# An adaptive-layernorm block on one Trainium2 core: matmuls of zeros in the opening, c loaded in rows, and another order of work in chunk 2

## The chip, the core and the metric

The kernel runs on one core of a Trainium2 chip. The core has five engines that run their own instruction streams: TensorE (PE in the profile; its weight loads are PEld), VectorE (DVE), ScalarE (ACT), GpSimd (POOL) and SyncE (SP), which here only issues transfers. TensorE writes its results to PSUM, eight banks from which VectorE and ScalarE read; everything else on the chip lies in SBUF. The engines wait for each other through semaphores, and each works through its own queue in order. The metric is the device time of one execution in microseconds (us).

## What is computed

A block with adaptive layernorm: from a condition row c six modulation rows are made; then a dilated sliding-window attention (32 heads of 18, eight keys two positions apart) and a gated feed-forward without a nonlinearity, each on a modulated layernorm and each added back through a gate row. 2048 rows of 576 values, bf16.

```python
mod = (silu(c) @ w_mod).reshape(1, 6, 1, -1)          # c (1, 576), w_mod (576, 3456)
sa, ca, ga, sb, cb, gb = (mod[:, k] for k in range(6))
h = layernorm(x) * (1 + ca) + sa
x = x + ga * A(h)                                     # A: wqkv (576, 1728), wo (576, 576)
h = layernorm(x) * (1 + cb) + sb
x = x + gb * B(h)

def A(x):                                             # W, dil = 8, 2
    q, k, v = split_heads(x @ wqkv)                   # 32 heads of 18
    idx = arange(S)[:, None] - arange(W) * dil        # masked where idx < 0
    attn = softmax(einsum(q, k[idx]) * 18 ** -0.5)
    return einsum(attn, v[idx]) @ wo

def B(x):                                             # w_gate, w_up (576, 4608), w_down (4608, 576)
    return ((x @ w_gate) * (x @ w_up)) @ w_down
```

## The kernel before

**Tiling.** The rows are cut into eight chunks of 256 (`CH`), each of two halves (`ST` = 2, index `j`) of 128 rows. The 576 columns are five tiles of 128 (`KT`); the fifth overlaps or is padded. The feed-forward works on five groups of row tiles, `GROUPS`: tiles 0 to 1 (chunk 0 alone), then 2 to 5, 6 to 9, 10 to 12, 13 to 15. For each group `gate_up` streams w_gate and w_up in nine blocks of 512 columns, and `down` streams w_down.

**Order.** Everything is under a manual schedule (`tc.manual_schedule`): each engine carries out its instructions in the order in which the Python text issues them. The order of the opening is written out by hand at the end of the main function; from the first `gate_up` on, attention for later chunks is spread as background pieces between the feed-forward's matmuls.

**The opening.** The steps up to the first feed-forward matmul are:

- Loads go out on SyncE in one order: x of chunk 0 by halves (L176), the weights of modulation rows 0 and 1 (`wmA`, through `load_wm` and `load_k`, L167 and L168), three pieces of wqk, x of chunk 1, wv, x of chunk 2, modulation rows 3 and 4 (`wmB`, four loads), wo in four pieces (L816), modulation row 2 (`wmC`, in a tile of the pool `wd`), x again for the residual, the rows 512 to 575 of w_gate and w_up (`wgr`), and five feed-forward blocks (L149). c is loaded on ScalarE's queue straight into columns, one value per partition (L183, L184).
- c is turned to silu(c) by Exp on ScalarE (L750) and three small VectorE operations (L754 to L756), giving `sc`. `ln_parts` makes the layernorm of a chunk in parts: `stat` (L233, L235) on VectorE, `rsq` (L238, L239) on ScalarE, `norm` (L243) on VectorE.
- `transposed` turns normalised rows by ten matmuls with the identity (L270) into PSUM; its result, when called, writes them with scale and shift to `hT` or `h2T`, three of five tiles on one of VectorE and ScalarE, two on the other (L259, L261).
- `mod_columns(wmA, 0)` computes two modulation rows as columns: two blocks of 25 matmuls with one moving column (L283), then VectorE adds into `modc` (L286, L288). `mod_row` computes the gate row `ga` for all partitions by ten matmuls (L295), and ScalarE copies it to `ga_bc` (L297, L298).
- `a_qj(j, g)` makes Q and K of one half of chunk 0, 45 matmuls of 128 columns a half (L338); `a_q(i, g)` makes group g of chunk i in matmuls of 256 columns, 45 in five groups. ScalarE copies both to qT and kT (L341 to L346). `a_v(i, j)` makes the value rows (L364, L366), ScalarE copies them (L368, L369), and GpSimd's queue writes them to DRAM (`vd`, L375), from where `b_ld` loads the shifted windows `vsh` (L383).
- Chunk 0's attention is done on its own path: products q·k on VectorE (`pj`, L778), sums per head on TensorE (`lj`, L786), softmax (`max_j`, `sum_j`), weights shifted to key positions by `to_keys` (L481 to L487, ScalarE copying `keyed`), weighted values on VectorE (`av_mul`, L496, four instructions), and their sums on TensorE (`av_sum(j, hf)`, L507, twenty matmuls a call into three PSUM tiles `po`). After the second call of a half ScalarE copies them to `oT` (L510 to L512).
- `b_wj(j)` multiplies half j by Wo (L521); `x1_half`, its result, forms the new residual x1 on VectorE (L527, L528) with the statistics of the second layernorm, whose rstd is `rsq2` and whose rows are `norm2`. Two calls of `transposed` write `h2T`, and then `gate_up` of group 0 begins (L621).

**PSUM.** In the opening a pool of five banks (`psp0`, tag "bank", function `ps`) serves everything but the `po` tiles, which have a pool of three (`pop`). Before the first feed-forward both pools are closed and one of eight banks is opened over them, so that the first tile of the new pool waits for the work of the old ones.

Of the kernel before, what the change touches and what calls it, by code (L numbers as in the profile page):

```python
# [7 lines left out]
BF = mybir.dt.bfloat16  # L8
F32 = mybir.dt.float32
ALU = mybir.AluOpType  # L10
# [33 lines left out]
def kernel(  # L44
# [49 lines left out]
    def js(j):  # L94
        return slice(j * P, (j + 1) * P)
# [75 lines left out]
    def load_wm(wm, bi, blk):  # L171
        return load_k(lambda p, k: wm[p, k, bi, :], w_mod, blk * D, D)

    x_in[0] = sp.tile([P, ST, D], BF, name="x_t0")
    for j in range(ST):
        nc.sync.dma_start(x_in[0][:, j, :], x_flat[js(j), :])  # L176
    c_bf = sp.tile([P, KT], BF, name="c_bf")
    nc.vector.memset(c_bf[:], 0.0)
    nc.vector.memset(eps[:], EPS)
    nc.vector.memset(addc[:, 0, :], 0.0)  # L180
    nc.vector.memset(addc[:, 1, :], 1.0)
    with nc.allow_non_contiguous_dma(reason="tiny column-layout load of c"):
        nc.scalar.dma_start(c_bf[:, 0:KF], c[0, 0:KF * P].rearrange("(m p) -> p m", p=P))  # L183
        nc.scalar.dma_start(c_bf[0:64, KF:KT], c[0, KF * P:D].rearrange("(m p) -> p m", p=64))  # L184
    nc.scalar.preload_act_table_set("natural_log_exp_and_others")
    wmA = sp.tile([P, KT, 2, D], BF, name="wmA", tag="wm")
    wmC = wdp.tile([P, FB, D], BF, name="wd")
    wmCr = x1p.tile([P, D], BF, name="x1")
# [8 lines left out]
    load_k(lambda p, k: wv[p, k, :], A_wqkv, 2 * D, D)  # L197


    nc.gpsimd.memset(ident[:], 0.0)  # L200
    nc.gpsimd.affine_select(out=ident[:], in_=ident[:], compare_op=ALU.not_equal, fill=1.0, base=0,
                            pattern=[[-1, P]], channel_multiplier=1)
    nc.gpsimd.memset(wqk[64:, KF, :], 0.0)
    for k in range(2):
        nc.gpsimd.memset(kTs[k][64:, KF, :], 0.0)
# [41 lines left out]
    def layernorm(src, tag):  # L247
        xn, stat, rsq, norm = ln_parts(src, tag)
        for j in range(ST):
            stat(j)  # L250

        def norms():
            for j in range(ST):
                norm(j)
        return xn, lambda: rsq(slice(0, ST)), norms

# [6 lines left out]
    def transposed(src, dst, cols, vi):  # L263
        n = P * len(cols)
        pA = ps([P, 3, n], BF, "tr_pA")
        pB = ps([P, 2, n], BF, "tr_pB")
        for m in range(KT):
            d = pA[:, m, :] if m < 3 else pB[:, m - 3, :]
            for c, j in enumerate(cols):
                nc.tensor.transpose(d[:, js(c)], src[:, j, m * P:(m + 1) * P], ident[:])  # L270

        def evict(first_on_dve=True):
            for m in range(KT):
                s = pA[:, m, :] if m < 3 else pB[:, m - 3, :]
                modulate(dst(m), s, m, vi + 1, vi, (m < 3) == first_on_dve)
        return evict

    def mod_columns(wm, pi):
        pm = ps([P, 2, KT], F32, "pm")
        for bi in range(2):  # L280
            for kt in range(KT):
                for m in range(KT):
                    nc.tensor.matmul(pm[:, bi, m:m + 1], lhsT=wm[:, kt, bi, col(m)], rhs=sc[:, kt:kt + 1],  # L283
                                     start=(bi == 0 and kt == 0 and m == 0), stop=(kt == KT - 1), skip_group_check=True)
        c01 = slice(2 * pi, 2 * pi + 2)
        nc.vector.tensor_tensor(modc[:, c01, 0:KF], pm[:, :, 0:KF], addc[:, :, 0:KF], ALU.add)  # L286
        for r in (slice(0, 64), slice(64, P)):
            nc.vector.tensor_tensor(modc[r, c01, KF:KT], pm[64:P, :, KF:KT], addc[64:P, :, KF:KT], ALU.add)  # L288

    def mod_row(wm, dst, sc_bc):  # L290
        pa = ps([P, 512], F32, "pa")
        pb = ps([P, 64], F32, "pb")
        for p_t, c0, c1 in ((pa, 0, 512), (pb, 512, D)):
            for kt in range(KT):
                nc.tensor.matmul(p_t[:], lhsT=sc_bc[:, kt, :], rhs=wm(slice(0, P), kt)[:, c0:c1],  # L295
                                 start=(kt == 0), stop=(kt == KT - 1))
        nc.scalar.copy(dst[:, 0:512], pa[:])  # L297
        nc.scalar.copy(dst[:, 512:D], pb[:])  # L298
# [49 lines left out]
    def a_q(i, g):  # L348
        qk_tiles(i, QGRP[g], slice(0, CH), nc.scalar.copy)
        if g == 2:  # L350
            a_halo(i)
# [394 lines left out]
    x0 = x_in.pop(0)  # L746
    xn0, stat0, rsq0, norm0 = ln_parts(lambda j: x0[:, j, :], "a")
    aa[0] = dict(xn=xn0)
    e_f = sp.tile([P, KT], F32, name="e_f")
    nc.scalar.activation(e_f[:], c_bf[:], ACTF.Exp, scale=-1.0)  # L750
    for j in range(ST):
        stat0(j)
        rsq0(slice(j, j + 1))
    nc.vector.tensor_scalar_add(e_f[:], e_f[:], 1.0)  # L754
    nc.vector.reciprocal(e_f[:], e_f[:])
    nc.vector.tensor_tensor(sc[:], c_bf[:], e_f[:], ALU.mult)  # L756
    for j in range(ST):
        norm0(j)
    a_tiles(0)
    a_halo(0)  # L760
    hT0 = aa[0]["hT"]
    nc.gpsimd.tensor_copy(sc_bc[:], sc[:, :, None].to_broadcast([P, KT, P]))
    ev = [transposed(xn0, lambda m, j=j: hT0[:, m, js(j)], (j,), 0) for j in range(ST)]
    mod_columns(wmA, 0)
    for e in ev:
        e()
    for j, g in ((0, 0), (1, 0), (0, 1), (0, 2), (1, 1), (1, 2)):
        a_qj(j, g, nc.scalar.copy)
    a_ln(1)
# [28 lines left out]
    def sum_j(j):  # L798
        ss = small.tile([P, H], F32, name="ssj")
        nc.vector.tensor_reduce(ss[:], dd0[:, j].rearrange("p w h -> p h w"), axis=AX.X, op=ALU.add)  # L800
        nc.vector.reciprocal(ss[:], ss[:])
        nc.vector.tensor_tensor(attn0[:, :, j], dd0[:, j].rearrange("p (a w) h -> p a w h", a=2),
                                ss[:, None, None, :].to_broadcast([P, 2, 4, H]), ALU.mult)

    def behind(dma, load):
        tc.add_manual_dep(dma.ins, load.ins.name, SYNC, reason="value rows go first")
# [1 line left out]
    load_x(2)  # L808
    wmB = sp.tile([P, KT, 2, D], BF, name="wmB", tag="wm")
    nc.gpsimd.memset(wmB[64:, KF, :, :], 0.0)  # L810
    load_wm(wmB, 0, 3)
    load_wm(wmB, 1, 4)
    for dd4 in range(4):
        nk = (DH - dd4 + 3) // 4
        wsrc = bass.AP(A_wo.tensor, A_wo.offset + dd4 * D, [[DH * D, H], [4 * D, nk], [1, D]])
# [40 lines left out]
    max_j(1)  # L856
    a_q(1, 4)
    mod_columns(wmB, 1)
    aa[2]["norm"]()
    sum_j(1)  # L860
    for j in range(ST):
        a_v(1, j)
    a_t(2, False)
    mod_row(lambda p, k: wmC[p, k, :] if k < KF else wmCr[p, :], ga_bc, sc_bc)
    for j in range(ST):
        to_keys(j)
    av_mul(0, 0)
    av_mul(0, 1)
    a_q(2, 0)
    av_sum(0, 0)  # L870
    av_mul(1, 0)
    a_q(2, 1)
    av_sum(0, 1)
    av_mul(1, 1)
    xn2, stat2, rsq2, norm2 = ln_parts(lambda j: x1[0][j], "b")
    ht, _ = h2_of(0)
    av_sum(1, 0)
    x1_half = b_wj(0)
    x1_half(stat2)
    rsq2(slice(0, 1))  # L880
    a_q(2, 2)
    av_sum(1, 1)
    norm2(0)
    a_q(2, 3)
    x1_half = b_wj(1)
    x1_half(stat2)
    rsq2(slice(1, 2))
    transposed(xn2, lambda m: ht[:, m, js(0)], (0,), 2)()
    norm2(1)
    a_q(2, 4)  # L890
    for j in range(ST):
        a_v(2, j)
    transposed(xn2, lambda m: ht[:, m, js(1)], (1,), 2)()
    behind(b_ld(1, 0), wgu_in[3])
    behind(b_ld(1, 1), wgu_in[4])
    load_res(1)
# [75 lines left out]
```

## Time and profile before

| | us |
|---|---|
| Time, median of 3 runs (lowest, highest) | 569.56 (569.03, 569.99) |
| The profiled execution, its own time | 569.6 |
| Its span, first to last instruction | 567.7 |
| TensorE busy (share of the span) | 547.7 (96%) |
| TensorE weight loads busy | 325.1 (57%) |
| VectorE busy | 327.9 (58%) |
| ScalarE busy | 250.4 (44%) |
| GpSimd busy | 69.5 (12%) |
| First matmul | 6.32 |
| First Q/K matmul of chunk 0 | 11.79 |
| First value matmul of chunk 0 | 19.51 |
| First feed-forward matmul | 57.39 |

All positions are counted from the first instruction of the span. A line of the timeline gives start, duration, engine, line of the kernel, operation, output and input by their names in the program, shape, count, and in brackets the idle time before it with what ended it. Instructions that overlap on an engine are counted once in its busy time. A matmul's duration contains its passage through the array, so matmuls that follow each other overlap, and their spacing is shorter than their duration. Durations come from one execution; the median is that of runs of their own.

### The profile page before, as it was taken

The numbers are of one execution on the slowest core, as the hardware profiler recorded it, in microseconds if no ns is written. First come the engines' busy times: TensorE is split into PE (matmuls) and PEld (weight loads), VectorE is DVE, ScalarE is ACT, GpSimd is POOL, SyncE is SP. The second block draws the span as 40 slices with busy tenths as digits, with TensorE's granted clock in tenths as the row PEclk, the third lists the DMA queues.
The fourth block names the chain that finished last, engine by engine and source line by source line (L and its number), as shares of the span: only waits on it lengthen the run. The fifth ranks groups of instructions, "written<-read, shape, count | busy, mean of one in ns | idle before, by whom it ended". The sixth has DMA issues, their size and how long they took to land.

```text
span 567.7 us, 14223 instructions
## 1 busy us (share of the span) xinstructions
PE 547.7 (96%) x5995; PEld 325.1 (57%) x5995; DVE 327.9 (58%) x787; ACT 250.4 (44%) x576; POOL 69.5 (12%) x105
## 2 busy tenths in 40 slices
PE   3998999999999999999999999999999999999996
PEld 3876888566444445656444444665556555566563
DVE  4785879995768687341767777406727614322203
ACT  2554566254455653323355554231466511455500
POOL 7000401231000000131100100122000022000022
PEclk9999999999999999999999999999999999999999
DMA  9998999948424864282443765338556565565063
GB/s 250 279 257 261 301 315 304 298 142 292 143 80 156 290 199 145 84 271 85 147 149 126 232 224 156 118 109 286 162 163 202 185 195 175 181 206 168 1 172 111
DMA packets 72448, 108.14 MB, mean 190 GB/s; under 512 B 4768, under 2 KB 62320, under 8 KB 72256
## 3 DMA queue, kind: packets, MB, share of 16 engines
q1 hardware_dynamic: 60608, 61.42, 35.1%
q0 software_dynamic: 11168, 45.81, 25.4%
q8 instruction: 47, 0.77, 0.6%
q14 instruction: 17, 0.14, 0.1%
q10 hardware_dynamic: 608, 0.00, 0.1%
HBM read 102.78 MB, written 4.44 MB: 189 GB/s over the span
## 4 chain that ended last, share of the span: by engine, by line
PE 55%; issue 31%; DMA 6%; POOL 3%; DVE 2%; ACT 2%; SPq 1%; POOLq 0%
PE pg L621 15%; PE pu L621 12%; PE acc L688 11%; PE pq L338 6%; PE pv L364 2%; POOL wd L164 2%; DMA wd<-in_B_w_down_dram 2%; DMA wgu<-in_B_w_up_dram 2%; PE accr L692 2%; PE pw L538 2%; DMA wqk<-in_A_wqkv_dram 1%; PE lg L399 1%; PE po L507 1%; DMA vd<-v_sb 1%; PE tr_pA L270 1%
## 5 line engine op out<-in xcount | busy, mean ns | idle before, releaser
L621 PE MATMUL pg<-h2T,wgu 64*128 64x512 bf16 (+2 forms) x1440 | 277.3, 333 | 0.0
L621 PE MATMUL pu<-h2T,wgu 64*128 64x512 bf16 (+2 forms) x1440 | 276.0, 333 | 0.0
L621 PEld LDWEIGHTS <-wgu 64*128 64x128 bf16 x2880 | 141.5, 94 | 107.0 <-issue 0.5
L645 ACT CAST u_sb<-pu 128x512 bf16<-128x512 f32 (+2 forms) x180 | 90.1, 501 | 136.5 <-PE pg L621 134.9
L688 PE MATMUL acc<-wd,hh 128*128 128x512 bf16 (+1 forms) x596 | 146.9, 368 | 0.4 <-DMA wd<-in_B_w_down_dram 0.3
L650 DVE TENSOR_TENSOR hh<-g_sb,u_sb 128x512 bf16<-128x512 bf16 (+2 forms) x180 | 66.3, 370 | 99.6 <-ACT g_sb L646 97.7
L692 PE MATMUL accr<-wd,hh 128*128 128x64 bf16 x576 | 101.0, 193 | 0.0
L646 ACT CAST g_sb<-pg 128x512 bf16<-128x512 f32 (+2 forms) x180 | 91.4, 508 | 0.0
L688 PEld LDWEIGHTS <-hh 128*128 128x128 bf16 x596 | 55.8, 98 | 58.2 <-issue 1.7
L164 POOL DMA_DIRECT2D wd<-in_B_w_down_dram x45 | 33.8, 751 | 282.6 <-PE accr L692 229.9
L621 PE MATMUL pg<-h2T,wgr 64*128 64x512 bf16 (+2 forms) x180 | 60.2, 335 | 1.2 <-ACT h2T L261 1.2
L621 PE MATMUL pu<-h2T,wgr 64*128 64x512 bf16 (+2 forms) x180 | 60.2, 335 | 0.3 <-ACT u_sb L645 0.3
L692 PEld LDWEIGHTS <-hh 128*128 128x128 bf16 x576 | 52.4, 98 | 3.2 <-issue 0.9
L338 PE MATMUL pq<-hT,wqk 128*128 128x256 bf16 (+1 forms) x405 | 47.8, 272 | 1.9 <-DMA wqk<-in_A_wqkv_dram 1.5
L389 DVE TENSOR_TENSOR prod<-qT,kT 128x1280 bf16<-128x1280 bf16 x56 | 44.8, 819 | 2.8 <-PE lg L399 2.8
L449 DVE TENSOR_TENSOR vsh<-vsh,attn 128x1152 bf16<-128x1152 bf16 x56 | 41.0, 752 | 0.0
L338 PEld LDWEIGHTS <-wqk 128*128 128x128 bf16 x405 | 36.3, 104 | 8.2 <-DMA wqk<-in_A_wqkv_dram 1.6
L259 DVE TENSOR_SCALAR h2T<-tr_pA,modc 128x256 bf16<-128x256 bf16 (+1 forms) x30 | 9.6, 376 | 37.1 <-PE tr_pA L270 37.1
L383 POOL DMA_DIRECT2D vsh<-vd x14 | 12.7, 906 | 134.9 <-DVE o_sb L460 88.0
L621 PEld LDWEIGHTS <-wgr 64*128 64x128 bf16 x360 | 18.1, 94 | 17.9 <-issue 5.5
L341 ACT CAST qT<-pq 128x512 bf16<-128x512 f32 x16 | 9.3, 582 | 35.7 <-PE pq L338 35.7
L456 DVE TENSOR_TENSOR vsh<-vsh 128x1152 bf16<-128x1152 bf16 x28 | 20.5, 751 | 0.0
(155 smaller groups left out, 441.6 us busy)
## 6 DMA issues: line engine op xcount, KB each, us to landing
wd<-in_B_w_down_dram POOLq DMA_DIRECT2D x45, 576.0 KB, 4.5
wgu<-in_B_w_gate_dram SPq DMA_DIRECT2D x45, 512.0 KB, 3.8
wgu<-in_B_w_up_dram SPq DMA_DIRECT2D x45, 512.0 KB, 5.0
vsh<-vd POOLq DMA_DIRECT2D x14, 1152.0 KB, 7.2
x_r<-in_A_x_dram SPq DMA_DIRECT2D x8, 288.0 KB, 6.2
out_dram<-x SPq DMA_DIRECT2D x15, 144.0 KB, 4.4
x_t<-in_A_x_dram SPq DMA_DIRECT2D x7, 288.0 KB, 5.9
vd<-v_sb POOLq DMA_DIRECT2D x14, 144.0 KB, 2.3
```

Of the source, the lines that this page charges most:

```text
L164: return nc.gpsimd.dma_start(wb[:], B_w_down[r0:r0 + FB * P, :].rearrange("(k p) n -> p k n", p=P))
L338: nc.tensor.matmul(pq[:, gi, :], lhsT=wqk[:, kt, m * P:(m + 1) * P], rhs=hT[:, kt, cols], start=(kt == 0), stop=(kt == KT - 1))
L383: return nc.gpsimd.dma_start(vsh[:].rearrange("p w d h -> p w (d h)"), vsrc)
L389: nc.vector.tensor_tensor(prod[:], aa[i]["qT"][:], aa[i]["kT"][:, :, off:off + CH], ALU.mult)
L449: nc.vector.tensor_tensor(v, v, at, ALU.mult)
L456: nc.vector.tensor_tensor(vsh[:, d], vsh[:, d], vsh[:, 4 + 2 * s:6 + 2 * s], ALU.add)
L621: return nc.tensor.matmul(bank[:, 0:N], lhsT=lhs, rhs=rhs, start=first, stop=last, skip_group_check=True)
L645: nc.scalar.copy(u[:, 0:N], pu[:, 0:N])
L646: nc.scalar.copy(g[:, 0:N], pg[:, 0:N])
L650: nc.vector.tensor_tensor(hh[:, f, 0:N], gu[0][:, 0:N], gu[1][:, 0:N], ALU.mult)
L688: nc.tensor.matmul(a[:], lhsT=hh[:, f, js(j)], rhs=wb[:, f % FB, cs], start=(f == 0), stop=(f == FT - 1))
L692: nc.tensor.matmul(accr[:, j, :], lhsT=hh[:, f, js(j)], rhs=wb[:, f % FB, 512:D], start=(f == 0 and j == 0), stop=(f == FT - 1), skip_grou ...
```

## The change

In the opening, a tile `zero` of zeros is set, and `run_idle(n)` issues n matmuls of 128 by 128 by 128 zeros into a tile of the pool `pop` that nobody reads. It is called with 12 and 24 before the first transposes, 16 between the two blocks of the first `mod_columns`, and 20 before Q and K of chunk 0. c is loaded in five rows of up to 128 values; one matmul with the identity, with the rows as the stationary operand, turns it into columns in PSUM (`c_col`), from where ScalarE and VectorE read it; the identity is therefore built first on GpSimd. The three small operations for `sc` now stand between the statistics of the two halves. `wmB` comes as one pair of loads with twice the width. In chunk 2 the normalisation of the second half stands behind `sum_j(1)`, `mod_row` behind the weighted values, all four `av_sum` calls before `b_wj(0)`, both `b_wj` before the first transposes of the second layernorm with `norm2(0)` between them, and the second `a_v(2, j)` behind the last transposes.

```diff
-    c_bf = sp.tile([P, KT], BF, name="c_bf")
-    nc.vector.memset(c_bf[:], 0.0)
+    zero = sp.tile([P, P], BF, name="zero")
+    nc.vector.memset(zero[:], 0.0)
+    idle = pop.tile([P, 2, CH], F32, name="po")
+
+    def run_idle(n):
+        for _ in range(n):
+            nc.tensor.matmul(idle[:, 0, 0:P], lhsT=zero[:], rhs=zero[:], start=True, stop=True, skip_group_check=True)
+
+    c_row = sp.tile([KT, P], BF, name="c_row")
+    nc.vector.memset(c_row[:], 0.0)
...
-        nc.scalar.dma_start(c_bf[:, 0:KF], c[0, 0:KF * P].rearrange("(m p) -> p m", p=P))
-        nc.scalar.dma_start(c_bf[0:64, KF:KT], c[0, KF * P:D].rearrange("(m p) -> p m", p=64))
+    nc.scalar.dma_start(c_row[0:KF, :], c[0, 0:KF * P].rearrange("(m p) -> m p", p=P))
+    nc.scalar.dma_start(c_row[KF:KT, 0:D - KF * P], c[0:1, KF * P:D])
...
     def mod_columns(wm, pi):
         pm = ps([P, 2, KT], F32, "pm")
         for bi in range(2):
+            if pi == 0 and bi == 1:
+                run_idle(16)
...
+    run_idle(12)
+    c_col = ps([P, KT], F32, "c_col")
+    nc.tensor.matmul(c_col[:], lhsT=c_row[:], rhs=ident[0:KT, 0:KT], start=True, stop=True)
     e_f = sp.tile([P, KT], F32, name="e_f")
-    nc.scalar.activation(e_f[:], c_bf[:], ACTF.Exp, scale=-1.0)
-    for j in range(ST):
-        stat0(j)
-        rsq0(slice(j, j + 1))
+    nc.scalar.activation(e_f[:], c_col[:], ACTF.Exp, scale=-1.0)
+    stat0(0)
+    rsq0(slice(0, 1))
     nc.vector.tensor_scalar_add(e_f[:], e_f[:], 1.0)
     nc.vector.reciprocal(e_f[:], e_f[:])
-    nc.vector.tensor_tensor(sc[:], c_bf[:], e_f[:], ALU.mult)
+    nc.vector.tensor_tensor(sc[:], c_col[:], e_f[:], ALU.mult)
+    stat0(1)
+    rsq0(slice(1, 2))
...
+    run_idle(24)
     ev = [transposed(xn0, lambda m, j=j: hT0[:, m, js(j)], (j,), 0) for j in range(ST)]
     mod_columns(wmA, 0)
     for e in ev:
         e()
+    run_idle(20)
     for j, g in ((0, 0), (1, 0), (0, 1), (0, 2), (1, 1), (1, 2)):
         a_qj(j, g, nc.scalar.copy)
...
-    load_wm(wmB, 0, 3)
-    load_wm(wmB, 1, 4)
+    load_k(lambda p, k: wmB[p, k, :, :].rearrange("p k b n -> p k (b n)") if k != KF else wmB[p, k, :, :].rearrange("p b n -> p (b n)"), w_mod, 3 * D, 2 * D)
...
-    aa[2]["norm"]()
+    aa[2]["norm"]((0,))
     sum_j(1)
+    aa[2]["norm"]((1,))
     for j in range(ST):
         a_v(1, j)
     a_t(2, False)
-    mod_row(lambda p, k: wmC[p, k, :] if k < KF else wmCr[p, :], ga_bc, sc_bc)
     for j in range(ST):
         to_keys(j)
     av_mul(0, 0)
     av_mul(0, 1)
+    mod_row(lambda p, k: wmC[p, k, :] if k < KF else wmCr[p, :], ga_bc, sc_bc)
     a_q(2, 0)
     av_sum(0, 0)
     av_mul(1, 0)
-    a_q(2, 1)
     av_sum(0, 1)
     av_mul(1, 1)
     xn2, stat2, rsq2, norm2 = ln_parts(lambda j: x1[0][j], "b")
     ht, _ = h2_of(0)
+    a_q(2, 1)
     av_sum(1, 0)
+    a_q(2, 2)
+    av_sum(1, 1)
     x1_half = b_wj(0)
     x1_half(stat2)
     rsq2(slice(0, 1))
-    a_q(2, 2)
-    av_sum(1, 1)
-    norm2(0)
     a_q(2, 3)
     x1_half = b_wj(1)
+    norm2(0)
     x1_half(stat2)
     rsq2(slice(1, 2))
+    a_q(2, 4)
     transposed(xn2, lambda m: ht[:, m, js(0)], (0,), 2)()
     norm2(1)
-    a_q(2, 4)
-    for j in range(ST):
-        a_v(2, j)
+    a_v(2, 0)
     transposed(xn2, lambda m: ht[:, m, js(1)], (1,), 2)()
+    a_v(2, 1)
```

## The prediction

> **What bounds the kernel now.** I read the page's slices first, then TensorE's timeline of the opening.
>
> ```profile
> PE   3998999999999999999999999999999999999996
> ```
>
> After the first slice of 14.2 us TensorE is 80 to 90% busy or more. Its idle stretches after the feed-forward begins at 57.39 us add up to about 1 us (the longest 0.50), so whatever brings that point forward shifts the rest, and a gain must be found ahead of it.
>
> ```profile
> 6.32 0.50 PE L270 MATMUL tr_pA<-ident,ln_xn 128*128 128x128 bf16 x3 [6.32 <-DVE ln_xn L243]
> ...
> 9.42 0.83 PE L283 MATMUL pm<-sc,wmA 128*128 128x1 bf16 x25 [1.08 <-DMA wmA<-in_w_mod_dram]
> 11.79 7.88 PE L338 MATMUL pq<-hT,wqk 128*128 128x128 bf16 x90 [1.54 <-DMA wqk<-in_A_wqkv_dram]
> 19.51 1.23 PE L364 MATMUL pv<-wv,hT 128*128 128x504 bf16 x5
> ```
>
> Start, duration, engine, line, waits in brackets: 6.32 us without work, then two waits for weights, then 90 Q/K matmuls of chunk 0.
>
> ```profile
> L338 PE MATMUL pq<-hT,wqk x90: 219/311/314, 11.8 to 19.5; 128*128 128x128 bf16 x90
> ```
>
> ```profile
> 12.00:13.00 1.00, 1.00 (x11) 0.83 (x10) 0.46 (x2) 0.02 (x1) 0.00 (x0) 1.00 1.10 288
> ...
> 18.00:19.00 1.00, 1.00 (x21) 1.00 (x19) 0.07 (x1) 0.67 (x2) 0.00 (x0) 1.00 1.09 311
> ```
>
> One shape has two speeds (min/median/max ns): 311 ns with starts 107 ns apart up to 17.39 us, 219 ns with starts 56 ns apart after. The windows (first bracket: TensorE's instructions) show 11 and 21 in a microsecond, though their granted clock says 1.00 both times (third number from the end), so this ramp is seen in durations only. It came 5.6 us after the unbroken run began at 11.79.
>
> VectorE in this stretch, then the end of the opening on TensorE and ScalarE:
>
> ```profile
> 15.16 0.82 DVE L233 BATCH_NORM_STATS2 ln_statsa<-x_t 128x6 f32<-128x288 bf16 x2 [2.69 <-DMA x_t<-in_A_x_dram]
> ...
> 18.93 1.29 DVE L778 TENSOR_TENSOR prodj<-qT,kT 128x640 bf16<-128x640 bf16 x3 [1.78 <-ACT kT L346]
> 20.76 1.19 DVE L243 TENSOR_SCALAR ln_xn<-x_t,ln_mva,ln_rstda 128x576 bf16<-128x576 bf16 x4 [0.53 <-ACT ln_rstda L239]
> ```
>
> ```profile
> 50.07 1.47 PE L521 MATMUL pwj<-wo,oT 128*128 128x288 bf16 x10 [1.09 <-ACT oT L510]
> ...
> 57.39 0.27 PE L621 MATMUL pg<-h2T,wgr 64*128 64x256 bf16 x1 [1.16 <-ACT h2T L261]
> ```
>
> ```profile
> 48.42 0.29 ACT L238 ACTIVATE ln_rstdb<-ln_mvb,eps 128x1 f32<-128x1 f32 x1 [4.53 <-DVE ln_mvb L235]
> ...
> 49.64 0.38 ACT L510 CAST oT<-po 128x256 bf16<-128x256 f32 x1
> ```
>
> From 20.76 to 36.5 VectorE has no idle time worth naming: it sets the pace there, and its start inherits the end of the Q/K matmuls through kT and the rstd behind it in ScalarE's queue. At 48.42 ScalarE waits 4.53 us for the row statistics, and the copies of oT that Wo needs stand behind that wait, though their sums ended at 47.9.
>
> **The change, part by part.** All times are on the clock of the profile before.
>
> *c in rows.* The two column loads of c go as two-byte elements:
>
> ```profile
> q10 hardware_dynamic: 608, 0.00, 1.3%
> ```
>
> 608 packets held 1.3% of 24 us on each of 16 transfer engines: 0.31 us, which the saturated queues behind (DMA share above 1.0 from 7 us on) get back. wqk thus lands near 11.45 instead of 11.75, x of chunk 1 near 14.8 instead of 15.1. c itself landed at 4.54; x's first half took 2.2 us from issue, so I put c at 3.75 (issue 1.5). Then matmul 0.3, Exp 0.21, three small VectorE operations 0.57 as before: sc is ready at 4.9 instead of 5.93. As they stand ahead of the second half's statistics, those run 4.95 to 6.0 (before 4.38 to 5.45); the second half is normalised by 7.15 (before 6.98) and its transposes end at 7.65, the first modulation block at 8.35. Upper end: c as late as before, then all this 0.8 later. ident is built first on GpSimd (0.5 us), which moves wmA's memset to about 2.4, long before its use.
>
> *Zeros.* Per block n x 107 ns cold, n x 56 ns fast. 12 run from 1.05 to 2.3 in idle time; 24 from 4.05 to 6.6 delay the first transposes by 0.25 us, hidden as the second half comes at 7.15 anyway; 16 stand between the two modulation blocks in the 1.25 us hole behind 8.35; 20 stand ahead of Q/K. From 4.05 on TensorE is then never idle for long. By the row (5.6 us) the speed changes at 9.65. So the 16 end at 9.87, the second modulation block at 10.56 (before 10.10), and hT's third tile 1.56 us behind, as before, at 12.12; the 20 end at 11.68. The 90 matmuls, 56 ns each, take 5.04 us; held by hT they start in effect at 12.06 and end at 17.1, against 19.51: 2.4 us. wv (landing 17.1 and 17.46 before, 0.3 earlier now) just allows V to follow.
>
> The Trainium skill's page "TensorE: Matmul & The Clock Gate" (Part 1) has the speed decided over free-running windows of about 3.4 us, which would put the change 3.4 to 6.8 us behind the start, not at a fixed 5.6. By it the change falls between 7.45 and 10.9, and the gain between 2.65 and 2.25.
>
> *What follows.* VectorE's statistics of chunk 1 run 14.8 to 16.8, its products 16.8 to 18.1 (kT of the first half comes at 16.5), rstd is there at 17.1 + 1.25 (as 19.51 to 20.76 before) = 18.35: the busy stretch begins 2.4 us early, and its fixed work carries that to 36. Nothing it needs lands too late: of the loads issued by 20.5 us the last landed at 29, and is used at 36. Bounds of this part: 2.0 (c late, zeros slow) and 2.65 (limited by x of chunk 1 alone).
>
> *Chunk 2 and weighted sums*, on the old clock, the shift left out. Normalising half 1 of chunk 2 moves behind sum_j(1): its transposes go from 34.94 to 35.65, ScalarE's hT ends at 37.66 (before 37.06). But the 0.73 us of ga_bc copies no longer stand ahead of keyed, so the first weighted product starts at 37.98 (before 37.95): even. mod_row's 1.25 us of matmuls (35.50 to 36.73 before) run behind to_keys, in TensorE's wait for that product. The four sums start at 39.40, 40.65, 42.98 and 44.65, with Q/K groups 1 and 2 between, and end at 45.76 (before 47.72). Wo of half 0 starts at 45.76, later than its 44.84 before; Wo of half 1 follows at 48.07 with no wait (before 50.07). VectorE's x1 chains (2.73 us each) run 46.57 to 49.30 and, after rstd and norm2(0), 50.53 to 53.26 (before to 53.70). ScalarE then has rstd 0.52, kT group 4, h2T of half 0, V of half 0, h2T of half 1 and V of half 1, 3.75 us in a row. Moving the second V behind the last transposes adds a wait: the first feed-forward matmul waits for all earlier ScalarE work, its PSUM pool being new, and that now ends with the second V's copy: 57.1. So only 57.39 - 57.1 = 0.3 us is gained; the saved oT wait of 1.09 comes back in ScalarE's tail. Bounds: +1.1 (that wait is won whole) and -0.6 (one more V copy, 0.58, in the tail). The value copies' writes and the vsh loads behind them on GpSimd keep their place ahead of the feed-forward.
>
> *wmB in one pair of loads.* Same 1.3 MB, two issues of about 0.9 us together less on SyncE; each issue there waits for the landing eight issues earlier, so wo goes out about 1 us sooner behind saturated engines. wmB landed by 24 and is used at 31: nothing.
>
> **Sum.** 2.4 + 0.3 = 2.7 us off the span of 567.7, so 565.0. The profiled execution took 569.6, 1.9 more than its span and 0.04 over the median of 569.56: **566.9**. Own range by the bounds: 2.0 - 0.6 to 2.65 + 1.1, that is 568.2 to 565.8.
>
> **Rivals.**
> *The stream is too mixed to lift the speed early.* For: transposes and one-column modulation matmuls stand between the zeros, and before they did not lift it. Against: there they were 1.8 us of work with two long holes. Then all zeros run at 107 ns: second modulation block 10.75, the 20 to 12.9; counted from 10.75, the lift comes at 16.35: 32 matmuls cold, 58 fast, end 19.6. Gain -0.1 + 0.3: 569.4. The same page (Part 4) says transposes do not count as busy; by that rule this rival is right if the modulation matmuls do not count either, which no run here shows.
> *Slower: zeros do not count at all.* Q/K starts at 12.9 and its ramp of 5.6 us is paid whole: 1.1 us later everywhere from there, less 0.3: 570.4; with the second stage at its bad end 571.3. It decides as soon as the 20 end later than 11.79. Against: the 107 and 56 ns differ by time, not by line; no row ties them to the values, none excludes it.
> *The feed-forward cannot use it*, as its weights come too late. For: DMA is saturated until 50 us. Against: its share falls to 0.32 in 55 to 60 and the fifth block, issued by 46.8 with landings of 11.6 us, is needed near 73. Then 569.5.
>
> **How the numbers follow.** Forecast 0.74, mixed stream 0.10, zeros not counted 0.08, weights late 0.03, the rest unforeseen, half of it slower. A measurement here tells 0.2% (1.1 us) from no change. Faster: the forecast and some of the rest, 0.79; same: the mixed stream, the late weights and the mild end of the slower rival, 0.13; slower 0.08. The range goes from 565.6 to 569.0, which leaves out most of the rivals.
>
> **What would show it.** Q/K at 219 ns throughout, beginning near 11.7 and ending near 17.1; VectorE's first products near 16.8; feed-forward starting near 54.7 (57.1 - 2.4) behind ScalarE's copy of V. Wrong if the Q/K row still shows 311 ns, if zeros last beyond 12 us, or if the feed-forward waits for something other than ScalarE or starts away from 53.6 to 56.

## The result, and the profile after

| | median of runs | runs, spread | profiled execution, span |
|---|---|---|---|
| before | 569.14 us | 22, 567.44 to 570.48 | 569.6, 567.7 |
| changed | 567.88 us | 22, 566.29 to 569.78 | 567.9, 565.9 |

The ratio is 0.9977, 95% interval 0.9967 to 0.9987: 1.3 us faster, where 2.7 were forecast. The measured median lies inside the forecast's range of 565.6 to 569.0, but a microsecond above its 566.9. The kernel before, too, has a lower median over 22 runs than over the three at hand for the forecast (569.14 in place of 569.56). In a later session one run of the changed kernel took 2582 us; it is left out of every mean below.

The timeline of TensorE in the changed kernel, opening (start, duration, both in us, then engine, line, operation, count, and in brackets what it waited for):

```profile
3.85 2.74 PE L183 MATMUL po<-zero 128*128 128x128 bf16 x24
...
8.08 1.05 PE L183 MATMUL po<-zero 128*128 128x128 bf16 x16
...
10.02 1.28 PE L183 MATMUL po<-zero 128*128 128x128 bf16 x20
11.65 5.51 PE L347 MATMUL pq<-hT,wqk 128*128 128x128 bf16 x90 [0.35 <-DVE hT L266]
17.00 1.24 PE L373 MATMUL pv<-wv,hT 128*128 128x504 bf16 x5
```

24 zeros take 2.74 us, but the next 16 only 1.05: the speed changed between them, during the transposes at 7.32 us. All 90 Q/K matmuls are fast (5.51 us; 7.88 before), and the value matmuls begin at 17.00 in place of 19.51. The gain of the opening, 2.5 us, is there.

The same timeline at the end of chunk 2's preparation, where the feed-forward begins (L630):

```profile
48.47 1.22 PE L373 MATMUL pv<-wv,hT 128*128 128x504 bf16 x5
49.66 0.32 PE L375 MATMUL pvr<-wv,hT 128*128 128x72 bf16 x5
51.81 0.50 PE L277 MATMUL tr_pA<-ident,ln_xn 128*128 128x128 bf16 x3 [1.82 <-DVE ln_xn L250]
52.10 0.42 PE L277 MATMUL tr_pB<-ident,ln_xn 128*128 128x128 bf16 x2
52.49 2.26 PE L373 MATMUL pv<-wv,hT 128*128 128x504 bf16 x5
54.55 0.50 PE L375 MATMUL pvr<-wv,hT 128*128 128x72 bf16 x5
55.54 0.27 PE L630 MATMUL pg<-h2T,wgr 64*128 64x256 bf16 x1 [0.49 <-ACT v_sb L378]
```

The first value block takes 1.22 us, the second, of the same shape, 2.26. Between them TensorE is idle for 1.82 us. The windows of that stretch (first bracket: TensorE busy and its instructions; third number from the end: granted clock) and the page's row of clock slices say why:

```profile
49.00:50.00 1.00, 0.99 (x9) 0.39 (x6) 0.93 (x4) 0.00 (x0) 0.00 (x0) 1.00 1.11 351
50.00:51.00 1.00, 0.00 (x0) 0.00 (x0) 0.96 (x4) 0.27 (x1) 0.00 (x0) 1.00 0.87 283
51.00:52.00 1.00, 0.19 (x3) 0.20 (x4) 0.96 (x4) 0.97 (x5) 0.00 (x0) 0.85 0.29 98
52.00:53.00 1.00, 1.00 (x7) 0.59 (x6) 0.65 (x3) 1.00 (x5) 0.00 (x0) 0.50 0.12 42
...
55.00:56.00 1.00, 0.51 (x11) 0.54 (x12) 0.00 (x0) 0.49 (x2) 0.21 (x1) 0.95 0.00 0
```

```profile
PEclk9998999999999999999999999999999999999999
```

The granted clock falls to 0.50 at 51.70 us (0.85 is the mean of 0.70 us at 1.00 and 0.30 at 0.50) and returns at 55.11, 3.41 us later; the 8 in the fourth slice is this fall. ScalarE's copy of that slow value block is what the feed-forward waits for:

```profile
54.79 0.58 ACT L377 CAST v_sb<-pv 128x504 bf16<-128x504 f32 x1 [1.05 <-PE pv L373]
```

The path can be cut at four marks on TensorE's timeline, the same for every kernel below (all from the profiled executions, us):

| kernel | first V | V to first weighted sum | weighted sum to feed-forward | feed-forward to end of span | clock falls to 0.50 |
|---|---|---|---|---|---|
| before | 19.51 | 19.86 | 18.02 | 510.3 | no |
| changed | 17.00 | 19.81 | 18.73 | 510.3 | 51.7 to 55.1 |

Ahead of the feed-forward the change wins 2.5 in the opening and loses 0.7 in the third stretch, where a gain of 0.3 was forecast. The feed-forward itself is unchanged.

### The profile page after: what moved, and what is told of

Same layout as the page of the kernel before. It is cut to its first block, busy times and chain, and to the rows that moved or that the text cites. A ratio compares the mean times of both kernels' runs of the same rounds, so it can differ in the third digit from the quotient of the medians.

```text
span 565.9 us, 14371 instructions
## 1 busy us (share of the span) xinstructions
PE 552.2 (98%) x6068; PEld 328.9 (58%) x6068; DVE 327.9 (58%) x788; ACT 250.9 (44%) x576; POOL 70.2 (12%) x105
## 4 chain that ended last, share of the span: by engine, by line
PE 87%; DVE 2%; ACT 1%; issue 0%; ACTq 0%
PE pg L630 27%; PE pu L630 22%; PE acc L697 21%; PE pq L347 4%; PE accr L701 3%; PE pw L547 2%; PE pv L373 2%; PE lg L408 2%; PE tr_pA L277 1%; PE oT_pA L478 0%; PE tr_pB L277 0%; PE pwr L545 0%; PE lt L424 0%; PE acc L728 0%; PE pvr L375 0%
## 5 line engine op out<-in xcount | busy, mean ns | idle before, releaser
L630 PE MATMUL pg<-h2T,wgu 64*128 64x512 bf16 (+2 forms) x1440 | 277.3, 333 | 0.0
L630 PE MATMUL pu<-h2T,wgu 64*128 64x512 bf16 (+2 forms) x1440 | 276.0, 333 | 0.0
L630 PEld LDWEIGHTS <-wgu 64*128 64x128 bf16 x2880 | 141.6, 94 | 106.9 <-issue 0.5
L697 PEld LDWEIGHTS <-hh 128*128 128x128 bf16 x596 | 55.8, 98 | 58.1 <-issue 1.7
L630 PE MATMUL pg<-h2T,wgr 64*128 64x512 bf16 (+2 forms) x180 | 60.3, 335 | 0.5 <-ACT v_sb L378 0.5
L630 PE MATMUL pu<-h2T,wgr 64*128 64x512 bf16 (+2 forms) x180 | 60.3, 335 | 0.3 <-ACT u_sb L654 0.3
L347 PE MATMUL pq<-hT,wqk 128*128 128x256 bf16 (+1 forms) x405 | 45.3, 261 | 0.9 <-ACT hT L268 0.4
L347 PEld LDWEIGHTS <-wqk 128*128 128x128 bf16 x405 | 33.9, 98 | 7.2 <-issue 0.7
L630 PEld LDWEIGHTS <-wgr 64*128 64x128 bf16 x360 | 18.1, 94 | 17.2 <-issue 4.7
L373 PE MATMUL pv<-wv,hT 128*128 128x504 bf16 x80 | 20.7, 391 | 0.1
```

What stands on the lines that cost most here:

```text
L347: nc.tensor.matmul(pq[:, gi, :], lhsT=wqk[:, kt, m * P:(m + 1) * P], rhs=hT[:, kt, cols], start=(kt == 0), stop=(kt == KT - 1))
L373: nc.tensor.matmul(pv[:], lhsT=hT[:, kt, js(j)], rhs=wv[:, kt, 0:VA * DH], start=(kt == 0), stop=(kt == KT - 1))
L630: return nc.tensor.matmul(bank[:, 0:N], lhsT=lhs, rhs=rhs, start=first, stop=last, skip_group_check=True)
L697: nc.tensor.matmul(a[:], lhsT=hh[:, f, js(j)], rhs=wb[:, f % FB, cs], start=(f == 0), stop=(f == FT - 1))
```

## The experiments

Two theories were set against each other. A: the reordered chunk 2 leaves a hole (a stretch in which TensorE has no matmul to run) that lets the clock fall, and this takes back about 1 us. B: with the opening faster, its weights land too late, and this is what is missing. Kernels are the changed one with the edit shown, unless said otherwise. The kernel before, run beside them, had medians of 569.06 (the first four), 569.12 (the next four), 569.10 (the next three) and 568.91 (the last).

**The parts of the change by themselves.** open_only keeps the opening and puts back the old order of chunk 2 (the whole block of moved lines); order_only is the kernel before with that block alone.

> The changed opening (zeros, c in rows, wide wmB) with the old order of chunk 2. Theory: the opening alone gives 2.5 us (in the changed kernel the first value matmul starts at 17.0 instead of 19.5), and TensorE's longest idle stretch in the old order, 1.2 us, leaves the clock at 1.00; so the first feed-forward matmul starts at 54.9 and the time is 2.5 us under the kernel before. Rival, the order of chunk 2 is what gained: the first feed-forward matmul stays near 57 and the time within 0.5 us of before.

> The old opening (no zeros, c in columns, four loads of wmB) with the new order of chunk 2. Theory: the new order gains 0.3 us at the most and leaves TensorE idle for 1.8 us ahead of the last transposes, which takes the granted clock to 0.50 for 3.4 us in most executions and costs 1.1 us; so the first feed-forward matmul starts near 58.2 and the time is 0.8 us over before, where the clock falls, and 0.3 under where it does not. Rival, the order gains as meant: 0.5 to 1.1 us under before.

open_only: 567.68 (ratio 0.9970, 0.9957 to 0.9983). order_only: 569.07 (1.0000, 0.9981 to 1.0019). So on the median the opening alone gives all of the gain, and the new order gives nothing. But order_only's runs split by mean clock: the six at 0.998 or more average 568.07, the six below 570.71, against 569.2 for the kernel before. Both are further out than expected (0.3 under and 0.8 over); for the slow ones the profiled run says why, as its fall lasts two windows of 3.41 us, for the others it stays open. The profiled execution shows 18.73 us from weighted sum to feed-forward, as the changed kernel, with the clock down from 54.3 to 61.2; open_only shows 18.04, as before, and no fall. open_only was 1.1 us slower than its expectation, and its profiled run tells of theory B:

```profile
15.78 2.92 PE L347 MATMUL pq<-hT,wqk 128*128 128x128 bf16 x45 [1.03 <-DMA wqk<-in_A_wqkv_dram]
18.59 1.24 PE L373 MATMUL pv<-wv,hT 128*128 128x504 bf16 x5
```

Half of the Q/K matmuls wait 1.03 us for a late piece of wqk, and V starts 1.6 later than in the changed kernel, for the same program up to there. Before, the slow matmuls would have hidden such a landing: 45 of them, 107 ns apart from 11.79, last until 16.6.

**The hole closed.** fill puts 32 zeros into it:

```diff
     a_v(2, 0)
+    idle = pop.tile([P, 2, CH], F32, name="po")
+    run_idle(32, idle)
     transposed(xn2, lambda m: ht[:, m, js(1)], (1,), 2)()
```

spread moves real work there:

```diff
-    a_q(2, 4)
     transposed(xn2, lambda m: ht[:, m, js(0)], (0,), 2)()
     norm2(1)
     a_v(2, 0)
+    a_q(2, 4)
     transposed(xn2, lambda m: ht[:, m, js(1)], (1,), 2)()
```

> The changed kernel with 32 more matmuls of zeros in TensorE's idle stretch ahead of the last transposes. Theory: the changed kernel loses 1.1 us to the clock at 0.50 from 51.7 to 55.1; with the stretch filled the clock stays at 1.00, five value matmuls take 1.2 us instead of 2.3, the first feed-forward matmul starts near 54.4 and the time is about 2.9 us under before. Rival, it is the wait itself that costs and not the clock: the first feed-forward matmul stays at 55.5 and the time at 1.3 to 1.8 us under before.

> The changed kernel with the last Q/K group of chunk 2 moved from ahead of the first transposes into the idle stretch ahead of the last ones. Theory: real work does what the zeros do, the stretch of 1.8 us becomes two of about 1.1 and 0.8, the clock stays at 1.00 in most executions, the first feed-forward matmul starts near 54.5 and the time is about 2.8 us under before. Rival, only the total of idle time in the window counts: two holes of the same sum take the clock down as one does, and the time stays at that of the changed kernel, 1.3 to 1.8 us under before.

```profile
49.39 1.95 PE L183 MATMUL po<-zero 128*128 128x128 bf16 x32
...
52.06 1.22 PE L373 MATMUL pv<-wv,hT 128*128 128x504 bf16 x5 [0.24 <-ACT h2T L268]
```

In fill's timeline the second value block takes 1.22 us again, and the third stretch is 17.70 us: 1.03 less than with the fall, and 0.32 less than before, which is the 0.3 forecast for the new order. spread shows 17.68, and in both the feed-forward again waits for ScalarE's last copy of V. So in single executions the fall is what the third stretch loses. The medians don't follow: fill 568.11 (0.9981, 0.9966 to 0.9996) and spread 567.36 (0.9967, 0.9956 to 0.9979) were expected 2.9 and 2.8 us under before and came 1.0 and 1.7 under, which is no more than the rivals had allowed, and fill is no faster than the changed kernel. In fill, 9 of 12 runs have a clock of 0.998 or more, and yet average 567.72, 0.9 above the changed kernel's runs at such a clock (below). What takes this is not shown. spread's profiled run has another fall, at 30.4 us, behind a stretch of one-column matmuls:

```profile
27.63 0.69 PE L801 MATMUL lgj<-ind,prodj 128*128 128x32 bf16 x10 [0.48 <-DVE prodj L793]
28.17 1.25 PE L347 MATMUL pq<-hT,wqk 128*128 128x256 bf16 x10
29.25 1.40 PE L292 MATMUL pm<-sc,wmB 128*128 128x1 bf16 x50
30.51 2.26 PE L373 MATMUL pv<-wv,hT 128*128 128x504 bf16 x5
```

TensorE is idle here for only 0.48 us; V to weighted sum is 20.90 instead of 19.8.

**The changed kernel once more, and its opening taken apart.** again is the changed kernel. no_zeros leaves out every run_idle. c_cols loads c in columns as before, with 36 zeros in place of 24 so that TensorE stays busy. wide_a:

```diff
-    load_wm(wmA, 0, 0)
-    load_wm(wmA, 1, 1)
+    load_k(lambda p, k: wmA[p, k, :, :].rearrange("p k b n -> p k (b n)") if k != KF else wmA[p, k, :, :].rearrange("p b n -> p (b n)"), w_mod, 0, 2 * D)
...
-            if pi == 0 and bi == 1:
-                run_idle(16)
+            if pi == 0 and bi == 0:
+                run_idle(10)
```

> The changed kernel once more, beside the three others on one chip. Theory (a hole of 1.8 us in TensorE's work near 50 us lets the granted clock fall for one stretch of 3.4 us in most executions, which costs 1.1 to 1.3 us): median 567.9; of its runs about three in four show a mean granted clock of 0.993 to 0.997 and a mean time near 568, the others 0.998 or more and a mean near 566.8. Rival (the fall costs nothing that ends last): both groups have the same mean within 0.4.

> The changed kernel without any of its zero matmuls (c in rows, the wide wmB load and the new order of chunk 2 stay). Theory (the zeros carry the gain of the opening, c in rows almost nothing): about 40 of the 90 Q/K matmuls of chunk 0 run at 311 ns as before, the first value matmul starts at 18.9 to 19.4 us instead of 17.0, the median is 568.7 to 569.1, level with the kernel before. Rival (c in rows brings a large part, by 576 small packets less and an earlier sc): value matmuls at 17.5 to 18.2, median 567.9 to 568.3.

> The changed kernel with c loaded in columns as before (the matmul that turns it goes, 36 zeros in place of 24 keep TensorE running to the first transposes). Theory (c in rows is worth little beside the zeros, as the second modulation block waits for its weights until 9.4 anyway): Q/K starts 0.0 to 0.4 us later than 11.65, value matmuls at 17.0 to 17.5, median 0.0 to 0.4 above the changed kernel on the same chip. Rival (c in rows is needed for the gain): sc late, Q/K after 12.3, median 0.8 or more above.

> The changed kernel with wmA (the two modulation blocks that the opening waits for) loaded in one pair of loads, rows of 2304 bytes in place of 1152; of the zeros, 10 stand ahead of the first modulation block in place of 16 between the blocks. Theory (with the matmuls fast, the landings of the weights bind the opening; in the trace of the changed kernel 2304-byte packets moved 336 bytes per ns, 1152-byte ones 271): wmA whole at about 8 us, everything behind it in the queue 0.8 to 1.0 earlier, Q/K starts at 10.9 to 11.2, value matmuls at 16.1 to 16.5, median 0.5 to 0.9 under the changed kernel on the same chip, and its runs scatter less. Rival (TensorE's own work and the modulation chain bind, the landings only look close): Q/K at 11.5 or later, median within 0.3 of the changed kernel.

*again*: 567.88 (0.9975, 0.9962 to 0.9989). Its profiled execution took 566.47 and had no fall, though the hole is the same:

```profile
49.46 0.32 PE L375 MATMUL pvr<-wv,hT 128*128 128x72 bf16 x5
51.60 0.34 PE L277 MATMUL tr_pA<-ident,ln_xn 128*128 128x128 bf16 x3 [1.81 <-DVE ln_xn L250]
...
52.28 1.22 PE L373 MATMUL pv<-wv,hT 128*128 128x504 bf16 x5 [0.23 <-ACT h2T L268]
```

```profile
50.00:51.00 1.00, 0.00 (x0) 0.00 (x0) 0.96 (x5) 0.45 (x3) 0.00 (x0) 1.00 0.93 300
51.00:52.00 1.00, 0.40 (x5) 0.34 (x6) 0.77 (x4) 1.00 (x4) 0.00 (x0) 1.00 0.44 149
```

What differs is where the hole falls. In every trace the changes of the clock lie whole multiples of 3.41 us apart, but this grid begins at another point in each execution. In the changed kernel's trace one window (48.28 to 51.70) holds nearly the whole hole; here a boundary at 50.52 cuts it in two. Over the 33 runs of the changed kernel in both sessions, the 8 at a clock of 0.998 or more average 566.8 us, the 25 below 568.2. (At 0.997 a run may be without a fall, as the end of each span, behind the last matmul, is at 0.50 too.) The rival (equal means) falls. The whole 1.4 us need not be the hole's, as other things can bring a fall too (best_gap below).

*no_zeros*: 571.19 (1.0026, 1.0005 to 1.0047), worse than either theory had it. The opening is as the theory said:

```profile
11.73 7.81 PE L337 MATMUL pq<-hT,wqk 128*128 128x128 bf16 x90 [1.43 <-DMA wqk<-in_A_wqkv_dram]
19.38 1.23 PE L363 MATMUL pv<-wv,hT 128*128 128x504 bf16 x5
```

So the zeros carry the opening's gain. The other loss goes with the hole: seven of 12 runs have a clock of 0.993 to 0.995, and average 572.0, the other five 568.4. In the profiled one the fall lasts two windows and reaches into the feed-forward:

```profile
55.00:56.00 1.00, 1.00 (x3) 0.30 (x2) 1.00 (x3) 1.00 (x4) 0.33 (x1) 0.50 0.08 27
...
57.00:58.00 1.00, 0.51 (x8) 0.44 (x8) 0.00 (x0) 0.70 (x2) 0.00 (x0) 0.50 0.11 42
58.00:59.00 1.00, 1.00 (x12) 0.81 (x11) 0.00 (x0) 0.00 (x0) 0.77 (x2) 0.50 0.00 0
...
60.00:61.00 1.00, 1.00 (x12) 0.85 (x10) 0.00 (x0) 0.00 (x0) 0.96 (x2) 0.50 0.66 152
```

In the microsecond at 57 TensorE is half empty, as the feed-forward waits for ScalarE's tail until 57.89; by the shares worked out in the last section this left the window that ends at 58.1 too thin, and the clock stays down through a second one. Feed-forward to end takes 512.4 instead of 510.3.

*c_cols*: 567.79 (0.9983, 0.9964 to 1.0001), V at 16.97: as the changed kernel. c in rows is worth nothing that this can tell (the interval is about 1 us to either side), once zeros run. Its opening also shows zeros at work alone:

```profile
1.07 5.09 PE L183 MATMUL po<-zero 128*128 128x128 bf16 x48 [1.07 <-DVE c_bf L186]
6.68 0.34 PE L278 MATMUL tr_pA<-ident,ln_xn 128*128 128x128 bf16 x3 [0.51 <-DVE ln_xn L251]
```

The zeros start 107 ns apart up to 5.81 us and 56 ns apart from there, ahead of the first transpose.

*wide_a*: 568.90 (0.9999, 0.9988 to 1.0010), 1.0 over again. Not what theory B forecast:

```profile
9.14 1.56 PE L291 MATMUL pm<-sc,wmA 128*128 128x1 bf16 x50 [0.99 <-DMA wmA<-in_w_mod_dram]
10.56 1.96 PE L183 MATMUL po<-zero 128*128 128x128 bf16 x20
12.31 6.17 PE L346 MATMUL pq<-hT,wqk 128*128 128x128 bf16 x90
18.32 1.23 PE L372 MATMUL pv<-wv,hT 128*128 128x504 bf16 x5
```

wmA came at 9.1, not 8.0 (wide rows did not bring it forward by what their packets promised), both blocks then run in a row, and the clock, lifted at 7.54, falls again from 10.96 to 14.37. Its rival (a median within 0.3 of the changed kernel) isn't met either. This kernel tests no landing, as nothing landed a microsecond earlier.

**What counts as work for the clock.** fill_thin puts 72 zero matmuls of one column where fill has 32 of 128:

```diff
-    run_idle(32, idle)
+    for _ in range(72):
+        nc.tensor.matmul(idle[:, 0, 0:1], lhsT=zero[:], rhs=zero[:, 0:1], start=True, stop=True, skip_group_check=True)
```

> The run fill again, but its 32 zero matmuls of 128 columns in the hole of chunk 2 become 72 of one column (about 25 ns apart in the modulation blocks, so again some 1.8 us of work without a gap). Theory (the granted clock counts how much TensorE really streams, and a matmul of one column counts for next to nothing, as in the run spread, where 50 one-column matmuls and a gap of 0.5 us were followed by the fall at 30.4): most runs have a mean clock of 0.997 or less as in the changed kernel, the profiled one shows the fall between 49 and 56 us unless the hole lies across two windows, median 567.8 to 568.3. Rival (any matmul counts as work): the fall is as rare as in fill (9 of 12 runs at 0.998 or more), with means near 567.7 or below.

```profile
50.14 1.94 PE L909 MATMUL po<-zero 128*128 128x1 bf16 x72
...
52.81 1.52 PE L373 MATMUL pv<-wv,hT 128*128 128x504 bf16 x5 [0.24 <-ACT h2T L268]
54.13 0.51 PE L375 MATMUL pvr<-wv,hT 128*128 128x72 bf16 x5
```

```profile
51.00:52.00 1.00, 1.00 (x44) 0.99 (x40) 1.00 (x6) 0.92 (x4) 0.00 (x0) 1.00 0.46 158
...
53.00:54.00 1.00, 1.00 (x5) 0.44 (x4) 1.00 (x3) 1.00 (x4) 0.35 (x1) 0.80 0.09 27
54.00:55.00 1.00, 0.64 (x6) 0.43 (x5) 0.82 (x2) 0.69 (x3) 0.19 (x1) 0.50 0.27 106
```

569.28 (0.9996, 0.9983 to 1.0009); only 3 of 12 runs reach a clock of 0.998, against 9 of 12 in fill. The profile calls TensorE 1.00 busy through the thin stretch, and the clock falls at 53.60 all the same. So one-column matmuls count for too little to hold it. The median is 1.0 above the top of what was expected and 1.4 above the changed kernel, which has the bare hole; the profiled run waits more for loads in the feed-forward (512.6 us to the end), but whether that is the cause is open.

**A version without falls?** best_fill and best_spread add to fill and spread two patches: 22 zeros at the start in place of 12, and 8 zeros between the one-column blocks of wmB. best_gap is best_spread with these 8 moved into the 0.48 us gap ahead:

```diff
     for w in range(4, 8):
+        if w == 6:
+            run_idle(8, idle1)
         lj(1, w)
```

> fill with two more patches against falls of the clock: 8 zero matmuls between the two blocks of one-column matmuls of wmB (near 29 us) and 22 in place of 12 zeros at the start. Theory (three places of thin work can each cost the clock for 3.4 us and about 1.1 us of time: the opening, the wmB blocks, the hole of chunk 2): mean clock 0.997 or more in at least 10 of 12 runs, first weighted sum to feed-forward 17.7 us, median 566.7 to 567.1, 2.0 to 2.4 under the kernel before. Rival (the scatter between runs of these kernels comes from the landing of loads in the opening and not from the clock): high clock throughout, but the median stays at 567.4 to 568.1.

> spread (the last Q/K group of chunk 2 moved into the hole) with the same two patches. Theory: mean clock 0.997 or more in most runs, first weighted sum to feed-forward 17.7 us, median 566.7 to 567.2. Rival (landings of the opening make the scatter): median 567.3 to 567.8 as spread had it.

> best_spread with its 8 zeros of the wmB stretch moved from between the two modulation blocks, where they held back VectorE's modulation columns (value matmuls of chunk 0 to first weighted sum 20.25 us in best_spread, 19.8 in the changed kernel), into the 0.48 us gap some 2 us earlier in which TensorE waits for a product of VectorE. Theory: that distance is 19.8 us again, first weighted sum to feed-forward stays 17.7, mean clock 0.997 or more in at least 9 of 12 runs, median 566.5 to 567.0, 2.0 to 2.6 under the kernel before. Rival (what is left over the best runs is the landing of loads, which no placing of zeros changes): high clock, distances as said, and still a median of 567.1 or more.

best_fill: 568.23 (0.9986, 0.9973 to 0.9999). best_spread: 567.08 over 6 runs (0.9959, 0.9945 to 0.9974). best_gap: 567.50 (0.9975, 0.9958 to 0.9993). The stretches came out as expected; of the medians only best_spread's did, and best_fill and best_gap were 1.1 and 0.5 above the top of what was expected, as high as their rivals had them or higher. best_fill reaches a clock of 0.997 in 11 of 12 runs and is still no faster than the changed kernel, so the falls alone do not set the median; best_gap reaches it in 7, where 9 were expected. There is a price for the 8 zeros between the blocks: V to weighted sum 20.25 in best_fill and best_spread, 19.78 in best_gap; weighted sum to feed-forward 17.67 to 17.70 in all three. What is left varies elsewhere. best_fill, whose clock is high in most runs, loses by late loads in its profiled execution: wmA and wqk in the opening, and a weight block of the feed-forward,

```profile
392.48 0.63 PE L701 MATMUL accr<-wd,hh 128*128 128x64 bf16 x16 [0.95 <-DMA wd<-in_B_w_down_dram]
```

so that feed-forward to end takes 511.1. best_gap's profiled execution falls in the opening:

```profile
9.68 0.78 PE L292 MATMUL pm<-sc,wmA 128*128 128x1 bf16 x25 [0.53 <-DMA wmA<-in_w_mod_dram]
10.32 2.13 PE L183 MATMUL po<-zero 128*128 128x128 bf16 x20
12.24 6.01 PE L347 MATMUL pq<-hT,wqk 128*128 128x128 bf16 x90
18.09 1.23 PE L373 MATMUL pv<-wv,hT 128*128 128x504 bf16 x5
```

wmA's second block was 0.53 us late; this hole and the two thin blocks lay in one window, the clock was 0.50 from 10.54 to 13.95, and V starts 1.1 late. Late loads thus cost twice, as a wait and through the clock. The intervals of best_spread, spread, open_only and the changed kernel overlap: best_spread has the lowest median, and none is shown to beat the change.

The table of the marks, for the runs named above (us):

| kernel | first V | V to weighted sum | to feed-forward | to end | fall |
|---|---|---|---|---|---|
| again | 16.82 | 19.78 | 17.70 | 510.2 | no |
| c_cols | 16.97 | 19.80 | 17.70 | 510.0 | no |
| open_only | 18.59 | 19.95 | 18.04 | 510.1 | no |
| order_only | 19.17 | 19.79 | 18.73 | 511.8 | 54.3 to 61.2 |
| no_zeros | 19.38 | 19.78 | 18.73 | 512.4 | 54.7 to 61.5 |
| fill | 16.58 | 19.79 | 17.70 | 510.9 | no |
| fill_thin | 17.32 | 19.81 | 17.99 | 512.6 | 53.6 to 57.0 |
| spread | 17.51 | 20.90 | 17.68 | 510.1 | 30.4 to 33.9 |
| wide_a | 18.32 | 19.79 | 17.69 | 511.3 | 11.0 to 14.4 |
| best_fill | 17.43 | 20.25 | 17.70 | 511.1 | no |
| best_spread | 16.81 | 20.25 | 17.67 | 510.0 | no |
| best_gap | 18.09 | 19.78 | 17.68 | 511.2 | 10.5 to 14.0 |

## Why the prediction was right, and where it was not

*The opening: right in mechanism and size.* Forecast 2.4, measured 2.5 (V at 17.00, forecast 17.1). c was there at 3.75, as forecast. The speed change came at 7.32, not at the 9.65 of the row: "5.6 us after the unbroken run began" was a coincidence of one trace. In the profiled executions with zeros it came between 4.9 and 9.6, always on the 3.41 us grid, which is what the Trainium skill's page "TensorE: Matmul & The Clock Gate" (Part 1) says of a free-running window; the traces agree. The range of 7.45 to 10.9 that the prediction gave for that rule counted from 4.05 and asked for a full window; with the same opening the change came at 6.55 in spread, as a window with about 0.8 of it filled was enough. The gain hardly depends on it, as hT and the weights then hold Q/K (in again the change came at 9.56, and V at 16.82), which is why the wrong rule still gave the right 2.4. The rivals "too mixed a stream" and "zeros do not count" fall: the clock came up by 9.6 in every trace that had zeros, in c_cols by zeros alone, and no_zeros, where they are missing, has V at 19.38.

*c in rows:* the 0.31 us of DMA and the earlier sc are not seen in the time (c_cols within 0.1 us of again, which can't tell 0.3). *wmB in one pair:* priced at nothing; it was not undone by itself.

*What follows: right.* VectorE's statistics of chunk 1 ran from 15.05, its products from 16.95 (forecast 14.8, 16.8), and V to the first weighted sum stayed at 19.8 us, so the shift is passed on whole.

*Chunk 2: right without the fall, 0.7 wrong with it.* The first Wo block started at 43.20 (forecast 45.76, less 2.5 for the measured shift, 43.26), and the wait for ScalarE's last copy of V came as described. Where the clock stays up, the stretch gains 0.32 (18.02 to 17.70; forecast 0.3). The step that failed is the cost of moving the second V behind the last transposes. It was priced as a wait and a tail of ScalarE, but it also opens the 1.8 us hole in TensorE's work, and what a hole does to the clock was not priced, though the forecast lived on the reverse of it in the opening. It costs 1.03 us (18.73 against 17.70) in an execution with the fall; 25 of the 33 runs have a clock at which there can be one.

*The sum.* From the one profiled execution of before, 569.6 - 2.5 - 0.3 = 566.8 without the fall and 567.8 with it; the two profiled executions of the changed kernel took 566.47 and 567.9. But that execution of before lies 0.46 above the median of the 22 runs, so it is in part luck that the 8 runs without a fall average the forecast's time: they are 2.4 us under before, not 2.7. The median lacks 1.4 us of the forecast's gain. The fall's 1.03 and these 0.46 add up to about that, but this is arithmetic: fill, with the fall mostly gone, did not win the 1.03 back. Late landings (theory B) are shown for single executions, as in open_only and best_fill; how much of the medians' missing gain they take was not separated.

*The other rival:* the feed-forward used its earlier start (510.3 us both times), so late weights did not hold it back as a whole.

## What to carry to other kernels

Work that keeps TensorE streaming had a value of its own here: before moving matmuls off a spot, look at what that leaves in the 3.4 us around it, and put full matmuls, not thin ones, into a hole like the 1.8 us here. Judge such a change by many executions and by the mean clock of each, since the same program gains 2.4 us in its runs at a high clock and 1.0 in the others. When a stage is sped up to the landing of its weights, a late landing that slow matmuls hid before shows in the time, as in open_only.

## What the runs showed of the hardware

*Thresholds of the clock.* For the first 60 us of the profiled executions of before, changed and all twelve, each grid window of 3.41 us was given a share, an estimate: the time in which its matmuls of 64 columns or more stream, overlaps counted once, over the window's length (0.42 ns per column at clock 1.00, as 256 columns start 108 ns apart; twice that at 0.50). At 0.50, none of the 24 windows with such matmuls and a share of up to 0.75 lifted the clock, and all 19 from 0.75 up did; the nearest two on either side (both in again) have 0.750 and 0.753, closer than the estimate can tell. At 1.00, no window above 0.37 (185 of them) let it fall, and 7 of 9 below did; the two that did not (c_cols, wide_a, near 30 us) were filled up with matmuls of 32 columns and of one, but so was the one in spread that did, at the same share of 0.32 as c_cols; what 32 columns count stays open. So a fall needs no idle window. The Trainium skill's page "TensorE: Matmul & The Clock Gate" ("Why this matters for your kernels") asks for gaps of no more than about 3 us; here 1.8 us was enough, and 0.5 us beside thin matmuls. The Trainium skill is not borne out in this, and the measurement decides. The shares explain the long falls too: the window after the first fall had a share of 0.71 in order_only and 0.75 in no_zeros, which stayed slow, and 0.84 in the changed kernel.

*Transposes count.* The Trainium skill, in Part 4 of that page, says that they do not count as busy in the same way. Here they do: in again, the window from 6.15 to 9.56 has a share of 0.75 with its ten transposes and 0.45 without, and it lifted the clock, as did those of fill_thin and open_only with 0.77 (0.47 without), while windows without transposes and with shares from 0.50 to 0.75 did not (wide_a, best_gap, again). Where the two differ, the measurement decides.

*The profile's "busy" is not the clock's.* Seventy-two one-column matmuls read as 1.00 busy and let the clock fall; and the granted clock reads 1.00 in the first microseconds of each trace, where matmuls of 128 columns start 107 ns apart, as they do later at 0.50, and the clock is in fact down.
